# Dealing out the rows of wq, and merging a load and a store, in a decode block bound by its loads

## The chip, the cores and the metric

The kernel runs on one core of a Trainium2 chip. A core has a matrix engine (TensorE, PE in the profile), VectorE (DVE), ScalarE (ACT), GpSimd (POOL) and SyncE (SP), an on-chip memory of 128 partitions (SBUF), accumulators for PE (PSUM), and 16 DMA engines that move data between the chip's main memory (HBM) and SBUF. SP and ACT each have a queue from which they issue DMA transfers. The metric is the time of one execution in microseconds of device time; runs are told by their median.

## The reference

One decode step of a transformer block in float32: two sequences (B = 2), one new token each, model width D = 512, 32 heads of 128, a cache of 8192 keys and values per head, and a gated feed-forward part of width 1792.

```
h  = x + attention(layernorm(x)) @ wo
     q = layernorm(x) @ wq                      (2 x 4096)
     scores = q . k_cache / sqrt(128), softmax over 8192 keys, then . v_cache
h2 = h + (silu(n @ w_gate) * (n @ w_up)) @ w_down,   n = layernorm(h)
```

The caches are 268 MB each, wq and wo 8.4 MB each, and the three feed-forward matrices 3.7 MB each. Every byte is read once, 564.66 MB in all. The output is 2 x 512 numbers.

## The kernel before, in words

There are three large buffers of 128 partitions x 64 KB: two for keys (`kslot`) and one for wq, values and wo (`vslot`). Attention goes in U = 32 rounds, each of two heads of one sequence: 64 partitions per head, 128 keys in each partition. In a round VectorE multiplies the keys by the query in two halves (L419) and sums each product (L428); the maximum is found (L436, L319, L372), ScalarE takes the exponential (L385), and PE multiplies with the values (L329) and sums the pieces (L341).

All loads are issued by SP in one list (`loads`, L142 to L197, issued at L578 to L581): wq, K0 in two halves, K1, V0, K2, V1 and so on, the last values, then wo (three transfers, `WO`), w_gate with w_up (`WF`), and w_down in five pieces (`WD`). A load whose buffer is still in use waits on SP for the last reader of that buffer (`after`, L202 to L206), so the list is strictly in order.

The opening: GpSimd builds the identity matrix `ident` (L209, L213). ScalarE waits for it and then issues the load of x (L219). VectorE builds `fold` and `quarter` from ident, normalizes x (`layernorm`, L233 to L256: statistics, a power on GpSimd, one `tensor_scalar` into `y`), and PE transposes `y` into four columns per sequence (L253). In this transposition the model index is split as (p c), 128 partitions by c = 4, because partition p of wq's buffer holds the four rows 4p to 4p + 3 of wq, 64 KB in one piece. GpSimd then fills its remaining constants (L261 to L268, `consts_done`). When wq has landed, 64 steps of PE compute the queries (L292); the last of these frees `vslot` for V0.

The close: when the last round's output is done, PE gathers the heads (L463) and multiplies with wo, 32 chunks c of 128 rows, in order (L478); before a chunk with which a transfer begins it waits for that transfer (L472 to L474). The residual is added (L487, L491), the sum is normalized again, `hT` receives the transposed rows in the first two of 32 columns (L500), and the gate and up products run with all 32 columns (L512), each waiting for its loads. PE adds the residual h1 to the result through a slice of ident (L530), and multiplies with w_down (L564). Four column blocks t of the result sit in four groups of 32 partitions; in each group the first two partitions are the two sequences. VectorE copies them to SBUF (L575), and two stores, one from SP and one from ACT, write one sequence each (L583 to L592). SP waits for both and clears the semaphores.

Of the kernel before, what the change touches and what calls it, by code (L numbers as in the profile page):

```python
# [5 lines left out]
OP = mybir.AluOpType  # L6
# [3 lines left out]
P = 128  # L10
# [3 lines left out]
class Program:  # L14
# [16 lines left out]
    def wait(self, engine, *points):  # L31
        for s, value in points:
            if self.known[engine].get(s, 0) < value:
                self.known[engine][s] = value
                self.steps[engine].append(lambda e, s=s, v=value: e.wait_ge(s, v))  # L35

    def do(self, engine, fn, sem=None, by=1):

        if sem is None:
            self.steps[engine].append(fn)  # L40
            return None
        self.count[sem] += by
        self.steps[engine].append(lambda e: fn(e).then_inc(sem, by))
        return sem, self.count[sem]
# [8 lines left out]
def decode_block(nc, x, k_cache, v_cache, wq, wo, w_gate, w_up, w_down, out):  # L53
    B, _, D = x.shape
    _, H, S, DH = k_cache.shape
    F = w_gate.shape[1]
    assert DH == P and B == 2 and D == 512 and F == 14 * P and H == 32 and S == 64 * P
    DC = D // P
# [4 lines left out]
    HP = P // 2  # L63
    NJ = S // HP
    U = B * H // 2
    MQ = H // 2
    HALF = (slice(0, HP), slice(HP, P))

# [8 lines left out]
    def sbuf(name, *shape, align=32):  # L77
        return nc.alloc_sbuf_tensor(name, list(shape), F32, align_bytes=align).ap()
# [6 lines left out]
    kslot = [sbuf(f"kslot{n}", P, SLOT, align=512) for n in range(2)]  # L85
    vslot = sbuf("vslot", P, SLOT, align=512)
    xs = sbuf("xs", B, D)
    ident = sbuf("ident", P, P)
    nscale = sbuf("nscale", 1, HP)
    mhalf = sbuf("mhalf", B, 1)  # L90
# [8 lines left out]
    hT = sbuf("hT", P, DC, 32)  # L99
# [13 lines left out]
    mv = sbuf("ln_mv", B, 2)  # L113
    ve = sbuf("ln_ve", B, 1)
    rstd = sbuf("ln_rstd", B, 1)
    y = sbuf("ln_y", B, D)
# [8 lines left out]
    yt = bank[3][:, : DC * B].rearrange("p (c b) -> p c b", b=B)  # L125
    oq_ps = bank[3][:, DC * B : DC * B + B * H].rearrange("p (b c) -> p b c", b=B)
    f_ps = bank[1][:, P : 2 * P]

    g = Program(nc)
    wait, do = g.wait, g.do  # L130


    s_dve, s_act, s_pe, s_pool = (g.sem(n) for n in ("dve", "act", "pe", "pool"))
    s_dve_pe, s_act_pe, s_v = (g.sem(n) for n in ("dve_pe", "act_pe", "v"))
    s_k = [g.sem(f"k{n}") for n in range(2)]

    def alone(name):
        return g.sem(name)
# [5 lines left out]
    loads = []  # L144
# [12 lines left out]
            sem = alone(f"{kind}{i}_{c}") if own else s_k[i % 2] if kind == "k" else s_v  # L157
            loads.append(((kind, i), c, t[:, c * n : (c + 1) * n], k_src(cache, i)[:, c * n : (c + 1) * n], sem))

    loads.append((("wq", 0), 0, vslot, wq.rearrange("(p c) m -> p (c m)", p=P), s_v))  # L160
    load_kv("k", 0, 2)
    for i in range(1, U):
        load_kv("k", i)
# [2 lines left out]


    wo_t = vslot
    WO = ((0, 20), (20, 8), (28, 4))
    for e, (c, n) in enumerate(WO):  # L170
        loads.append((
            ("wo", 0), e,
# [8 lines left out]
    for e, (c, n) in enumerate(WF):  # L181
        src, c0 = (w_gate, c) if c < DC else (w_up, c - DC)
# [20 lines left out]
    for i in range(1, U):  # L203
        after["v", i] = ("v", i - 1) if i < U - 1 else ("k", U - 2)
        if i > 1:
            after["k", i] = ("k", i - 2)  # L206


    p0 = do("gpsimd", lambda e: e.memset(ident, 0.0), s_pool)  # L209
    wait("gpsimd", p0)  # L210
    ident_done = do(
        "gpsimd",
        lambda e: e.affine_select(  # L213
            out=ident, in_=ident, compare_op=OP.not_equal, fill=1.0, base=0, pattern=[[-1, P]], channel_multiplier=1
        ),
        s_pool,
    )
    wait("scalar", ident_done)
    do("scalar", lambda e: e.dma_start(xs, x.rearrange("b s d -> (b s) d")), x_in := alone("x"), 16)  # L219
    p0 = do("gpsimd", lambda e: e.memset(sides, 0.0), s_pool)  # L220
    do("vector", lambda e: e.memset(nscale, -SCALE))
    half_done = do("vector", lambda e: e.memset(mhalf, -0.5), s_dve)
    wait("vector", ident_done)
# [6 lines left out]
    do("vector", lambda e: e.memset(opart, 0.0))  # L230


    def layernorm(src, ready):  # L233
        wait("vector", *ready)
        p = do("vector", lambda e: e.bn_stats(stats, src), s_dve)  # L235
        wait("vector", p)
        p = do("vector", lambda e: e.bn_aggr(mv, stats), s_dve)
        wait("vector", p)
        p = do("vector", lambda e: e.tensor_scalar(ve, mv[:, 1:2], EPS, None, op0=OP.add), s_dve)
        wait("gpsimd", p)  # L240
        p = do("gpsimd", lambda e: e.tensor_tensor(rstd, ve, mhalf, op=OP.pow), s_pool)
        wait("vector", p)
        p = do(
            "vector",
            lambda e: e.tensor_scalar(y, src, mv[:, 0:1], rstd, op0=OP.subtract, op1=OP.mult),
            s_dve,
        )
        normed = p
        wait("tensor", p, ident_done)
        for c in range(DC):  # L250
            p = do(
                "tensor",
                lambda e, c=c: e.transpose(yt[:, c, :], y.rearrange("b (p c) -> b c p", c=DC)[:, c, :], ident[:B, :B]),  # L253
                s_pe if c == DC - 1 else None,
            )
        return normed, p  # L256

    _, p = layernorm(xs, [(x_in, 16)])


    for t, value in (  # L261
        (sides[HALF[0], :, :W], 1.0),
        (sides[HALF[1], :, W:], 1.0),
        (pz, 0.0),
        (hT, 0.0),
    ):
        wait("gpsimd", p0)
        p0 = do("gpsimd", lambda e, t=t, value=value: e.memset(t, value), s_pool)  # L268
    consts_done = p0


    wait("vector", p)
    p = do("vector", lambda e: e.tensor_copy(xT, yt), s_dve)
# [10 lines left out]
    for n, (m, b) in enumerate((m, b) for m in range(0, MQ, 4) for b in range(B)):  # L284
# [3 lines left out]
        for c in range(DC):  # L288
            for k in range(2):
                p = do(  # L290
                    "tensor",
                    lambda e, ps=ps, c=c, k=k, m=m, b=b: e.matmul(  # L292
                        ps[HALF[k]],
                        xb[:, c * B + b, :],
                        wqv[:, c, k, m : m + 4, :],
                        start=(c == 0),
                        stop=(c == DC - 1),
                    ),
# [11 lines left out]
    base = g.count[s_pe]  # L310
# [99 lines left out]
    for i in range(U):  # L410
        m, b = divmod(i, B)
# [3 lines left out]
        for c in range(parts):  # L415
# [7 lines left out]
            if i and c == 1:  # L423
                recip(i - 1)
            wait("vector", mult)
            p = do(
                "vector",
                lambda e, kt=kt, s=scores[i % 2][:, c * n : (c + 1) * n]: e.tensor_reduce(s, kt, axis=AX.X, op=OP.add),  # L428
                s_dve,
            )  # L430
        freed["k", i] = p
        if i:
# [16 lines left out]
    p = do(  # L449
        "vector",  # L450
        lambda e: e.tensor_tensor(  # L451
            om,
            oT.rearrange("p h b -> p b h")[:, :, :, None].to_broadcast([P, B, H, NQ]),
            quarter[:, None, None, :].to_broadcast([P, B, H, NQ]),
            op=OP.mult,
        ),
        s_dve,
    )
    wait("tensor", p)
    for b in range(B):  # L460
        p = do(
            "tensor",
            lambda e, b=b: e.matmul(  # L463
                oq_ps[:, b, :], om[:, b].rearrange("p h q -> p (h q)"), fold, start=True, stop=True
            ),
            s_pe if b == B - 1 else None,
        )
    wait("scalar", p)
    p = do("scalar", lambda e: e.activation(oq.rearrange("p c b -> p b c"), oq_ps, AF.Copy), s_act)
    wait("tensor", p, zeroed)  # L470
    for c in range(H):
        for e_, (c0, n) in enumerate(WO):  # L472
            if c0 == c:
                wait("tensor", landed[("wo", 0), e_])  # L474
        t = c % 4
        p = do(
            "tensor",
            lambda e, c=c, t=t: e.matmul(  # L478
                wide[0][32 * t : 32 * t + B, :],
                oq[:, c, :],  # L480
                wo_t[:, c * D : (c + 1) * D],
                start=(c < 4),
                stop=(c >= H - 4),
            ),
# [4 lines left out]
    p = do("scalar", lambda e: e.activation(osb, wide[0], AF.Copy), s_act)  # L489
# [5 lines left out]
    h1 = rest[:B, :D]  # L495
# [1 line left out]
    wait("scalar", normed)  # L497
    h1_done = do("scalar", lambda e: e.activation(h1, attn, AF.Copy), s_act)
    wait("vector", yt_done)
    hT_done = do("vector", lambda e: e.tensor_copy(hT[:, :, :B], yt), s_dve)  # L500
    wait("tensor", hT_done)

    def project_f(first, ps):
# [20 lines left out]
    p = project_f(0, gate)  # L524

    wait("tensor", h1_done)
    for t in range(4):
        do(
            "tensor",
            lambda e, t=t: e.matmul(  # L530
                f_ps[32 * t : 32 * t + 32, :], ident[:B, :32], h1[:, t * P : (t + 1) * P], start=True, stop=False
            ),
        )
    sg = rest[:, D : D + FQ]
    wait("scalar", p)
    p = do("scalar", lambda e: e.activation(sg, gate, AF.Sigmoid), s_act)
    wait("vector", p)
    sg_done = do("vector", lambda e: e.tensor_mul(sg, gate, sg), s_dve)
    p = project_f(DC, up)
# [4 lines left out]
    p = do(  # L544
        "vector",
        lambda e: e.tensor_mul(
            gu.rearrange("p (c j) -> p j c", c=FB),
            up.rearrange("p (j c) -> p j c", c=FB),
            sg.rearrange("p (j c) -> p j c", c=FB),
        ),  # L550
        s_dve,
    )
    gT = rest[:, D + 2 * FQ : D + 3 * FQ]
    wait("vector", p)
    p = do("vector", lambda e: e.transpose(gT, gu), s_dve)
    wait("tensor", p)
    for c in range(FB):
# [3 lines left out]
        for t in range(4):  # L561
            p = do(
                "tensor",
                lambda e, c=c, t=t: e.matmul(  # L564
                    f_ps[32 * t : 32 * t + 32, :],
                    gT[:, c * 32 : (c + 1) * 32],
                    wd_t[:, c * D + t * P : c * D + (t + 1) * P],
                    start=False,
                    stop=(c == FB - 1),
                ),  # L570
# [7 lines left out]
    for item, e_, dst, src, sem in loads:  # L578
        if item in after:
            wait("sync", freed[after[item]])  # L580
        do("sync", lambda e, dst=dst, src=src: e.dma_start(dst, src), sem, 16)  # L581
    stored = []
    for b, engine in enumerate(("sync", "scalar")):  # L583
        wait(engine, res_done)
        stored.append(
            do(
                engine,
                lambda e, b=b: e.dma_start(out[b, 0, :].rearrange("(t m) -> t m", t=4), res[b::32, :]),
                alone(f"out{b}"),
                16,  # L590
            )
        )  # L592

    wait("sync", *stored)
    ids = sorted(s.num for s in g.sems)
    assert ids == list(range(ids[0], ids[-1] + 1))
    do("sync", lambda e: e.sem_clear(range(ids[0], ids[-1] + 1)))
# [39 lines left out]
```

## Time and profile before

| | us |
|---|---|
| median of 3 runs | 1309.95 (1309.79 to 1310.46) |
| the profiled execution | 1309.7 |
| its span, first to last instruction | 1308.4 |
| DVE busy | 1131.3 (86%) |
| PE busy | 434.1 (33%) |
| ACT busy | 80.4 (6%) |
| mean granted TensorE clock | 0.634 |

A DMA transfer is cut into packets, here one contiguous piece of a partition's row each; the 16 engines work through their packets side by side. A timeline row gives the start, the length, the engine, the line, the operation, the output and inputs, and in brackets how long the engine had been idle and what ended that. A row of DMA issues ends with the size in KB and the time from issue to landing. "SPq" and "ACTq" are the issuing sequencers.

### The profile page before, as it was taken

What the parts mean: (1) busy time and instruction counts of PE and PEld (TensorE: products, weight loads), DVE (VectorE), ACT (ScalarE), POOL (GpSimd) and SP (SyncE); (2) the same over time, 40 slices, a digit from 0 to 9 for tenths busy, and PEclk for the clock granted to TensorE, in tenths of its full rate; (3) what the DMA queues carried; (4) which work ended last, traced back from release to release, by engine and by line L of the source; (5) the groups of instructions that cost most, each with busy time, mean ns of one, the idle gap of its engine ahead of it and who ended that gap; (6) DMA issues with size and microseconds to landing.
All of it is one profiled execution on the core that took longest, in us unless ns stands there. A gap on an engine that the chain in (4) does not pass through costs nothing.

```text
span 1308.4 us, 6704 instructions
## 1 busy us (share of the span) xinstructions
PE 434.1 (33%) x2952; PEld 135.6 (10%) x2952; DVE 1131.3 (86%) x246; ACT 80.4 (6%) x271; POOL 2.9 (0%) x13
## 2 busy tenths in 40 slices
PE   3633223333223333311333321233332233332276
PEld 1210001011001011100101100001100010110022
DVE  1999988889888889988888988888998888898841
ACT  0100000000000000000000000000000000000010
POOL 0000000000000000000000000000000000000000
PEclk9865566666556666656666656666655666665578
DMA  9999999999999999999999999999999999999998
GB/s 403 440 437 439 427 447 423 443 423 445 421 445 425 441 435 431 443 427 443 423 445 421 445 425 441 433 433 443 427 441 425 441 425 441 429 439 435 431 423 371
DMA packets 11118, 564.79 MB, mean 432 GB/s; under 512 B 1242, under 2 KB 1250, under 8 KB 1636
## 3 DMA queue, kind: packets, MB, share of 16 engines
q1 hardware_dynamic: 11096, 564.67, 99.7%
q8 instruction: 5, 0.08, 0.0%
q14 instruction: 5, 0.04, 0.0%
q10 hardware_dynamic: 12, 0.01, 0.0%
HBM read 564.66 MB, written 0.00 MB: 432 GB/s over the span
## 4 chain that ended last, share of the span: by engine, by line
DMA 53%; DVE 45%; PE 1%; SPq 0%; issue 0%; DVEq 0%
DMA kslot<-in_A_k_cache_dram 48%; DVE kslot L419 22%; DVE s L428 22%; DMA kslot<-in_A_v_cache_dram 3%; DMA kslot<-in_B_w_down_dram 3%; PE opart L329 1%; DVE gm L372 0%; SPq L581 0%; DVE r L398 0%; PE bank L564 0%; DVE m L436 0%; DVE kslot L575 0%; DVEq L35 0%
## 5 line engine op out<-in xcount | busy, mean ns | idle before, releaser
L419 DVE TENSOR_TENSOR kslot<-kslot,qsb 128x8192 f32<-128x8192 f32 x64 | 555.6, 8681 | 119.5 <-DMA kslot<-in_A_k_cache_dram 119.5
L428 DVE TENSOR_REDUCE s<-kslot 128x64 f32<-128x8192 f32 x64 | 555.2, 8675 | 0.1
L329 PE MATMUL opart<-vslot,pz 128*8 128x512 f32 x1984 | 285.3, 740 | 246.5 <-DMA vslot<-in_A_v_cache_dram 246.5
L321 PE MATMUL bank<-gm,nscale 1*64 1x1 f32 x64 | 11.8, 250 | 358.4 <-DVE gm L372 358.4
L329 PEld LDWEIGHTS opart<-vslot,pz 128*8 128x8 f32 x1984 | 55.3, 104 | 450.4 <-DMA vslot<-in_A_v_cache_dram 249.1
L319 PE MATMUL bank<-ident,m 128*1 128x128 f32 x64 | 18.7, 395 | 168.1 <-DVE m L436 168.1
L321 PEld LDWEIGHTS bank<-gm,nscale 1*64 1x64 f32 x64 | 9.1, 199 | 374.4 <-DVE gm L372 374.4
L341 PE MATMUL bank<-rdiag,osb 128*128 128x2 f32 x256 | 33.7, 254 | 26.3 <-ACT osb L405 26.3
L400 ACT ACTIVATE rdiag<-fold,r 128x8 f32<-128x8 f32 x32 | 9.6, 301 | 484.6 <-DVE r L398 484.6
L379 ACT ACTIVATE nb<-bank 128x1 f32<-128x1 f32 x32 | 5.5, 171 | 551.6 <-PE bank L322 551.6
L341 PEld LDWEIGHTS bank<-rdiag,osb 128*128 128x128 f32 x256 | 31.0, 191 | 56.0 <-ACT osb L405 56.0
L292 PE MATMUL wide<-vslot,osb 128*64 128x512 f32 x128 | 29.9, 630 | 9.4 <-DMA vslot<-in_A_wq_dram 9.4
L324 PE MATMUL bank<-rs,sides 128*128 128x1 f32 x64 | 18.8, 363 | 41.5 <-ACT pz L385 41.5
L385 ACT ACTIVATE pz<-s,nb 64x128 f32<-64x128 f32 x64 | 25.5, 399 | 1.4
L405 ACT ACTIVATE osb<-opart 128x512 f32<-128x512 f32 x32 | 19.1, 597 | 72.4 <-PE opart L329 72.4
L324 PEld LDWEIGHTS bank<-rs,sides 128*128 128x128 f32 x64 | 16.1, 313 | 44.2 <-ACT pz L385 44.2
L319 PEld LDWEIGHTS bank<-ident,m 128*1 128x1 f32 x64 | 2.7, 81 | 171.6 <-DVE m L436 171.6
L292 PEld LDWEIGHTS wide<-vslot,osb 128*64 128x64 f32 x128 | 10.5, 146 | 28.0 <-issue 28.0
L385 ACT ACTIVATION_READ_ACCUMULATOR pz<-s,nb 64x1 f32 x64 | 11.8, 184 | 0.0
L322 PE MATMUL bank<-gm,nscale 1*64 1x1 f32 x64 | 11.8, 250 | 0.0
L235 DVE BATCH_NORM_STATS2 ln_stats<-attn 2x6 f32<-2x512 f32 x1 | 0.7, 686 | 11.4 <-PE attn L491 11.4
L451 DVE TENSOR_TENSOR om<-oT,quarter 128x256 f32<-128x256 f32 x1 | 0.4, 426 | 11.4 <-ACT oT L407 11.4
(60 smaller groups left out, 104.3 us busy)
## 6 DMA issues: line engine op xcount, KB each, us to landing
kslot<-in_A_k_cache_dram SPq DMA_DIRECT2D x2, 4096.0 KB, 35.8
vslot<-in_A_wo_dram SPq DMA_DIRECT2D x1, 5120.0 KB, 22.0
kslot<-in_B_w_gate_dram SPq DMA_DIRECT2D x1, 3584.0 KB, 31.7
kslot<-in_B_w_up_dram SPq DMA_DIRECT2D x2, 1792.0 KB, 37.5
vslot<-in_A_wo_dram SPq DMA_DIRECT2D x1, 2048.0 KB, 26.4
kslot<-in_B_w_down_dram SPq DMA_DIRECT2D x2, 1024.0 KB, 29.9
vslot<-in_A_wo_dram SPq DMA_DIRECT2D x1, 1024.0 KB, 28.4
kslot<-in_B_w_down_dram SPq DMA_DIRECT2D x1, 768.0 KB, 32.3
```

The source lines that it names most:

```text
L292: lambda e, ps=ps, c=c, k=k, m=m, b=b: e.matmul(ps[HALF[k]], xb[:, c * B + b, :], wqv[:, c, k, m : m + 4, :], start=(c == 0), stop=(c == D ...
L319: e.matmul(mrow, m1, ident, start=True, stop=True).then_inc(s_pe, 1)
L321: e.matmul(nb_ps[HALF[0]], nscale, gm[:, 0:1], start=True, stop=True)
L322: e.matmul(nb_ps[HALF[1]], nscale, gm[:, 1:2], start=True, stop=True).then_inc(s_pe, 1)
L324: e.matmul(den, sides.rearrange("p w a -> p (w a)"), rs, start=True, stop=True).then_inc(s_pe, 1)
L329: inst = e.matmul(opart[32 * t : 32 * t + 2 * W, :], pz[:, w, :], t_v[:, w * W * DH : (w + 1) * W * DH], start=(w < 4), stop=(w >= NW - 4),)
L341: inst = e.matmul(ot_ps, osb[:, a * DH : (a + 1) * DH], rdiag[:, a::W], start=(a == 0), stop=(a == W - 1))
L385: lambda e, k=k, h=h: e.activation(pz[h, :, k * W : (k + 1) * W], s[h].rearrange("p (w a) -> p w a", a=W), AF.Exp, bias=nb[h], scale=SCALE ...
L400: do("scalar", lambda e: e.activation(rdiag, diag, AF.Copy, scale=r))
L405: do("scalar", lambda e: e.activation(osb, opart, AF.Copy), s_act_pe)
L419: mult = do("vector", lambda e, kt=kt, qb=qb: e.tensor_tensor(kt, kt, qb, op=OP.mult), s_dve)
L428: lambda e, kt=kt, s=scores[i % 2][:, c * n : (c + 1) * n]: e.tensor_reduce(s, kt, axis=AX.X, op=OP.add),
```

## The change

- The source of the wq load is described as (i e c) with e = 16 and c = 4: partition 8e + i receives the four rows that begin at row 64i + 4e. Each partition still receives one contiguous piece of 64 KB. If the 16 DMA engines take eight consecutive partitions each, engine e begins 64 KB behind engine e - 1, and goes on 1 MB further at each of its eight rows; before, it began 512 KB behind and read on without a gap.
- To match, the first normalization writes `y` in the order (e i c). The second one is left as it is.
- ScalarE issues the load of x as its first act and no longer waits for ident.
- wo comes in two transfers, chunks 0 to 19 and 20 to 31, instead of three.
- The two sequences sit in columns 0 and 16 of hT's 32 (`LANE` = 16), and so in partitions 0 and 16 of each group of the result. A new constant `place`, built by GpSimd with a memset and a select, puts the residual there. One store from SP, of eight partitions 16 apart, replaces the two.

```diff
+    LANE = 32 // B
+    place = sbuf("place", B, 32)
-    loads.append((("wq", 0), 0, vslot, wq.rearrange("(p c) m -> p (c m)", p=P), s_v))
+    NE = 16
+    loads.append((("wq", 0), 0, vslot, wq.rearrange("(i e c) m -> e i (c m)", e=NE, c=DC), s_v))
-    WO = ((0, 20), (20, 8), (28, 4))
+    WO = ((0, 20), (20, 12))
+    do("scalar", lambda e: e.dma_start(xs, x.rearrange("b s d -> (b s) d")), x_in := alone("x"), 16)
     p0 = do("gpsimd", lambda e: e.memset(ident, 0.0), s_pool)
...
-    wait("scalar", ident_done)
-    do("scalar", lambda e: e.dma_start(xs, x.rearrange("b s d -> (b s) d")), x_in := alone("x"), 16)
     p0 = do("gpsimd", lambda e: e.memset(sides, 0.0), s_pool)
+    p1 = do("gpsimd", lambda e: e.memset(place, 0.0), s_pool)
...
-    def layernorm(src, ready):
+    def layernorm(src, ready, **sizes):
+        into = y.rearrange("b (e i c) -> b i e c", **sizes) if sizes else y
+        from_ = src.rearrange("b (i e c) -> b i e c", **sizes) if sizes else src
...
-            lambda e: e.tensor_scalar(y, src, mv[:, 0:1], rstd, op0=OP.subtract, op1=OP.mult),
+            lambda e: e.tensor_scalar(into, from_, mv[:, 0:1], rstd, op0=OP.subtract, op1=OP.mult),
...
-    _, p = layernorm(xs, [(x_in, 16)])
+    _, p = layernorm(xs, [(x_in, 16)], e=NE, c=DC)
...
+    wait("gpsimd", p1)
+    p0 = do(
+        "gpsimd",
+        lambda e: e.affine_select(
+            out=place, in_=place, compare_op=OP.not_equal, fill=1.0,
+            base=0, pattern=[[-1, 32]], channel_multiplier=LANE,
+        ),
+        s_pool,
+    )
     consts_done = p0
...
-    hT_done = do("vector", lambda e: e.tensor_copy(hT[:, :, :B], yt), s_dve)
+    hT_done = do("vector", lambda e: e.tensor_copy(hT[:, :, ::LANE], yt), s_dve)
...
-                f_ps[32 * t : 32 * t + 32, :], ident[:B, :32], h1[:, t * P : (t + 1) * P], start=True, stop=False
+                f_ps[32 * t : 32 * t + 32, :], place, h1[:, t * P : (t + 1) * P], start=True, stop=False
...
-    stored = []
-    for b, engine in enumerate(("sync", "scalar")):
-        wait(engine, res_done)
-        stored.append(
-            do(
-                engine,
-                lambda e, b=b: e.dma_start(out[b, 0, :].rearrange("(t m) -> t m", t=4), res[b::32, :]),
-                alone(f"out{b}"),
-                16,
-            )
-        )
-    wait("sync", *stored)
+    wait("sync", res_done)
+    rows = out.rearrange("b s (t m) -> t (b s) m", t=4)
+    stored = do("sync", lambda e: e.dma_start(rows, res[::LANE, :]), alone("out"), 16)
+    wait("sync", stored)
```

More of the change, by code (lines that the diff above doesn't have):

```diff
@@ L268, in decode_block @@
         p0 = do("gpsimd", lambda e, t=t, value=value: e.memset(t, value), s_pool)
+    wait("gpsimd", p1)
+    p0 = do(
+        "gpsimd",
+        lambda e: e.affine_select(
+            out=place,
+            in_=place,
+            compare_op=OP.not_equal,
+            fill=1.0,
+            base=0,
+            pattern=[[-1, 32]],
+            channel_multiplier=LANE,
+        ),
+        s_pool,
+    )
     consts_done = p0
```

## The prediction

> **What bounds the kernel now.** I read the page first: the slices of the span, the share of each DMA queue, and the chain that ended last.
>
> ```profile
> DMA  9999999999999999999999999999999999999998
> GB/s 403 440 437 439 427 447 423 443 423 445 421 445 425 441 435 431 443 427 443 423 445 421 445 425 441 433 433 443 427 441 425 441 425 441 429 439 435 431 423 371
> q1 hardware_dynamic: 11096, 564.67, 99.7%
> HBM read 564.66 MB, written 0.00 MB: 432 GB/s over the span
> DMA 53%; DVE 45%; PE 1%; SPq 0%; issue 0%; DVEq 0%
> ```
>
> The chain gives VectorE 45%, but that is only one way through work that waits on loads. The queue row says more: the sixteen DMA engines spend 99.7% of the whole span inside packets of SP's queue. So I cut the span into stretches. The columns are the stretch, its length, busy time by engine, the granted clock, the DMA share and GB/s. This view books a packet's bytes and its whole duration in the stretch where the packet starts, so in a stretch that holds exactly one start of each of the 16 engines the DMA share times the length is the mean duration of a packet.
>
> ```profile
> 100.00:600.00 500.00, 154.45 (x1040) 47.25 (x1040) 458.37 (x93) 28.89 (x104) 0.00 (x0) 0.61 1.00 434
> 600.00:1200.00 600.00, 177.40 (x1208) 55.23 (x1208) 543.08 (x109) 34.50 (x125) 0.00 (x0) 0.61 1.00 434
> 55.00:67.09 12.09, 0.00 (x0) 0.00 (x0) 12.06 (x2) 0.00 (x0) 0.00 (x0) 0.62 0.99 428
> 1.50:2.50 1.00, 0.00 (x0) 0.00 (x0) 0.89 (x3) 0.41 (x1) 0.11 (x1) 1.00 3.21 1049
> 4.50:5.50 1.00, 0.00 (x0) 0.00 (x0) 0.00 (x0) 0.00 (x0) 0.00 (x0) 1.00 2.42 1049
> 7.00:8.00 1.00, 0.00 (x0) 0.00 (x0) 0.00 (x0) 0.00 (x0) 0.00 (x0) 1.00 2.43 1053
> 1.79:1.80 0.01, 0.00 (x0) 0.00 (x0) 0.01 (x2) 0.00 (x0) 0.00 (x0) 1.00 21.67 6554
> 2.04:2.06 0.02, 0.00 (x0) 0.00 (x0) 0.02 (x1) 0.00 (x0) 0.00 (x0) 1.00 9.15 3277
> 2.10:2.20 0.10, 0.00 (x0) 0.00 (x0) 0.04 (x1) 0.10 (x1) 0.00 (x0) 1.00 5.88 1966
> 5.40:5.50 0.10, 0.00 (x0) 0.00 (x0) 0.00 (x0) 0.00 (x0) 0.00 (x0) 1.00 1.51 655
> ```
>
> Between 100 and 1200 us the DMA engines are busy 1.00 of the time at 434 GB/s. There is no hole for a compute step to close. 564.66 MB at 434 GB/s is 1301.1 us of the 1308.4. What is left, some 7 us, is the start, the end, and what the packets lose. That bounds any gain of this change to a few microseconds.
>
> The stretch 1.50 to 2.50 holds 1.049 MB, which is 16 packets of 65.5 KB: the first row of wq on every engine. They take 3.21 us each; the second ones (4.50 to 5.50) take 2.42, as do all later ones. So the start of wq loses 0.79 us per engine, once. Two narrow stretches single out the ends: the packet that starts at 1.79 to 1.80 takes 21.67 x 0.01 x 16 = 3.47 us, the one at 2.04 to 2.06 takes 9.15 x 0.02 x 16 = 2.93 us. Lost time on the DMA engines is lost for good, because nothing behind it is ever idle.
>
> **The change, part by part.**
>
> *wq's rows dealt out.* Same bytes, same 128 rows of 64 KB. Only the addresses at which the engines stand together change: 64 KB apart instead of 512 KB, and each engine then jumps 1 MB from row to row instead of reading on. The trace of before does not show the new pattern, so I bound it. Best: no first packet loses anything. The latest second packet starts in 5.40 to 5.50, while the latest first one starts by 2.20 and would then end by about 4.6: up to 0.9 us. Worst within the aim: nothing changes, 0, because every first packet is slow for being the first. Between: even the fastest lost 2.93 - 2.42 = 0.51, which I call common to a cold start; the part that differs between engines (up to 3.47 - 2.93 = 0.54) looks like engines in each other's way, and this is what other addresses can remove. The latest engine would then start its second packet at about 2.15 + 2.93 = 5.08 instead of about 5.45. I take -0.4 us, nearest to the row of the fastest packet. A loss is possible too and is a rival below.
>
> *x's load moved ahead.* ScalarE no longer waits for ident (its issue at 1.49 follows POOL's select, done at 1.46) and issues at about 0.8, beside SP's issue of wq.
>
> ```profile
> 0.73 0.40 SPq L581 DMA_DIRECT2D vslot<-in_A_wq_dram  x1
> 1.49 0.56 ACTq L219 DMA_DIRECT2D xs<-in_A_x_dram  x1
> 10.40 0.68 DVE L235 BATCH_NORM_STATS2 ln_stats<-xs 2x6 f32<-2x512 f32 x1 [7.75 <-DMA xs<-in_A_x_dram]
> 12.13 0.54 DVE L245 TENSOR_SCALAR ln_y<-xs,ln_mv,ln_rstd 2x512 f32<-2x512 f32 x1 [0.67 <-POOL ln_rstd L241]
> 1.17 0.29 POOL L213 TENSOR_SCALAR_AFFINE_SELECT ident<-ident 128x128 f32<-128x128 f32 x1 [0.24 <-POOL ident L209]
> 13.60 0.43 DVE L278 COPY osb<-xT 128x512 f32<-128x512 f32 x1
> 22.80 29.86 PE L292 MATMUL wide<-vslot,osb 128*64 128x512 f32 x128 [9.44 <-DMA vslot<-in_A_wq_dram]
> 1294.79 0.62 DVE L538 TENSOR_TENSOR kslot<-wide,kslot 128x448 f32<-128x448 f32 x1 [7.15 <-ACT kslot L536]
> 1298.73 0.91 DVE L546 TENSOR_TENSOR kslot<-wide,kslot 128x448 f32<-128x448 f32 x1 [3.32 <-PE wide L512]
> 1306.28 0.65 SPq L588 DMA_DIRECT2D out_dram<-kslot  x1
> 1306.29 0.61 ACTq L588 DMA_DIRECT2D out_dram<-kslot  x1
> ```
>
> Its 4 KB are the difference between 1053 and 1049 in the stretch 7.00 to 8.00; they now come before or among the first packets and cost the same there. Everything up to osb may finish some 7 us earlier, and that is worth nothing: osb is ready at 14.03, and the projection starts at 22.80 because wq lands last. The risk is wq's own issue. Two issues at once took 0.65 and 0.61 at the end, while SP's for wq took 0.40 alone; if ScalarE's goes first, wq starts up to 0.6 us later, and so does everything. At the end SP, 0.01 us ahead, shows no wait for ScalarE. Bounds 0 to +0.6; I take 0.
>
> *y permuted on its way out, place, hT.* The first normalization's last step writes the same 512 elements in another order. A permuted VectorE step of this kernel (L546, 0.91 us) against a plain one of the same size (L538, 0.62) says 1.5 times, so 0.54 becomes about 0.8; it lies in the 8.7 us between osb and wq, so 0. The memset and affine_select of place (L213's select of 128 columns took 0.29) and the later end of POOL's constants are first needed after the projection, at 52.7: 0. The copy into hT moves the same 8 elements per partition, and place has the shape of the slice of ident that it replaces: 0.
>
> *wo in two transfers.* One issue fewer, on a queue that then waits for the last scores anyway. Each engine loses eight 8 KB packets joined to eight 16 KB ones. The cost of a packet as such comes from a stretch with 2 KB packets only:
>
> ```profile
> 1304.62:1305.12 0.50, 0.28 (x12) 0.28 (x16) 0.00 (x0) 0.00 (x0) 0.00 (x0) 1.00 0.23 86
> vslot<-in_A_wo_dram SPq DMA_DIRECT2D x1, 2048.0 KB, 26.4
> vslot<-in_A_wo_dram SPq DMA_DIRECT2D x1, 1024.0 KB, 28.4
> 1250.53 1.28 SPq L581 DMA_DIRECT2D vslot<-in_A_wo_dram  x3
> 1274.05 8.23 PE L478 MATMUL wide<-vslot,oq 128*2 128x512 f32 x64 [0.32 <-ACT oq L469]
> 1279.11 0.10 PEld L478 LDWEIGHTS wide<-vslot,oq 128*2 128x2 f32 x4 [0.33 <-issue]
> 1287.47 0.17 DVE L500 COPY hT<-bank 128x8 f32<-128x8 f32 x1 [0.73 <-PE bank L253]
> 1288.40 5.75 PE L512 MATMUL wide<-kslot,hT 128*32 128x448 f32 x32 [0.97 <-DMA kslot<-in_B_w_gate_dram]
> 1296.89 1.71 PE L512 MATMUL wide<-kslot,hT 128*32 128x448 f32 x16 [0.75 <-DMA kslot<-in_B_w_up_dram]
> 1303.60 0.86 PE L564 MATMUL bank<-kslot 128*32 128x128 f32 x24 [0.77 <-DMA kslot<-in_B_w_down_dram]
> ```
>
> 86 / (0.23 x 16) = 23.4 GB/s per engine, against 434 / 16 = 27.1: 2 KB take 88 ns instead of 76, so about 12 ns per packet, and eight of them 0.1 us. Against it, a new wait on PE. Rows 20 to 27 of wo used to be covered by a transfer that landed at about 1251.0 + 26.4 = 1277.4 (three issues in 1.28, so 0.43 apart); now they wait for the last byte, at about 1251.4 + 28.4 = 1279.8. PE loads c = 20 (weights 41 to 44 of 64) at 1279.11, so it stalls about 0.7 us. Behind it: hT, done at 1287.64, while the gate product starts at 1288.40 because w_gate lands then (0.76 to spare); later w_up holds PE for 0.75 and w_down for 0.77. The stall is swallowed there; without that cover it would cost 0.7. Sum: -0.1, bounds -0.1 to +0.6.
>
> *One store.* The two stores run side by side, but not equally late:
>
> ```profile
> 1307.50:1307.70 0.20, 0.00 (x0) 0.00 (x0) 0.00 (x0) 0.00 (x0) 0.00 (x0) 0.50 0.04 10
> 1307.70:1307.80 0.10, 0.00 (x0) 0.00 (x0) 0.00 (x0) 0.00 (x0) 0.00 (x0) 0.50 0.00 0
> 1307.80:1307.90 0.10, 0.00 (x0) 0.00 (x0) 0.00 (x0) 0.00 (x0) 0.00 (x0) 0.50 0.09 21
> SPq L35 <- DMA out_dram<-kslot: 1.3, 1, 1.3
> ```
>
> 2 KB move between 1307.50 and 1307.70, and 2 KB more after 1307.80, although both were issued within 0.01 us. The later one ends SP's wait of 1.3 us. One store of 4 KB from SP moves with the first: -0.25 us, bounds -0.4 (1307.90 back to 1307.50) to 0 (twice the rows per engine, or a longer issue, could eat it).
>
> Sum against the profiled execution: 1309.7 (span 1308.4 and 1.3 around it) - 0.4 - 0.1 - 0.25 = 1308.95. The median of the runs shown lies 0.25 above that execution, so the forecast for the median is 1309.95 - 0.75 = **1309.2 us**. What a measurement of this kernel tells from no change is about 0.2%, 2.6 us, so this counts as no change.
>
> **Rivals.**
>
> *Nothing at the start.* The first packets are slow because they are first, not for their addresses. For it: all 16 lose at least 0.51 us, and from the second packet on the engines stand the same 512 KB apart and lose nothing (2.42). Against: the loss differs from 0.51 to 1.05 among packets that start within 0.4 us. Then only store and wo stay: 1309.95 - 0.35 = 1309.6. The same comes out if the change doesn't do what it says: that an engine takes eight consecutive partitions is assumed, and if it takes others, the new order still puts engines megabytes apart at the start. [...]
>
> *Slower: the new jumps cost on every row.* If engines in step 64 KB apart, each jumping 1 MB, hinder one another as much as the first packets did, and don't drift apart, all eight rows of wq take 3.21 instead of 2.42: 7 x 0.79 = 5.5 us more, 1309.95 + 5.5 - 0.35 = 1315.1. It decides the sign from 2.6 us, about four slow rows of eight. For it: 3.21 is what engines in step can cost. Against: it heals after one row here. [...]
>
> *x ahead of wq.* ScalarE's issue delays SP's by 0.25 to 0.6 us, at the very point where nothing can make it up: 1309.2 + 0.25 to 0.6, 1309.5 to 1309.8, or 1310.2 where the start gains nothing either.
>
> **How the numbers follow.** Forecast, with a gain of 0.2 to 0.9 at the start: 0.50 (1308.6 to 1309.4). Nothing at the start: 0.30 (1309.5 to 1309.7). x ahead: 0.12 (up to 1310.2). Slower: 0.08, of which nearly all is beyond 2.6 us. To be faster by over 0.2% all bounds together (0.9 + 0.1 + 0.4) fall short by more than 1 us; 0.02 is left for what I have not seen. Which DMA engine is caught by an instruction fetch can shift the last landing by some tenths, so the range is 1308.2 to 1310.5; only the slower rival lies wholly outside.
>
> **What would show it.** Right: in the first microsecond of packets the mean falls from 3.21 to about 2.9, x's statistics start near 3 us, wq's product starts at 22.4 instead of 22.80, one store, and SP's last wait near 1.0. A PE wait on wo of about 0.7 at c = 20, and waits on w_gate shortened by as much. Wrong: first packets at 3.2 again; second and later packets of wq above 2.42; a first packet of wq starting later than 2.20; a DMA share below 1.00 anywhere before 1300.

## The result: 21 us slower, all of it in one load

The changed kernel takes 1330.91 us (median of 5 runs, 1330.75 to 1331.21), the kernel before in the same comparison 1309.79 (1309.66 to 1310.46). The ratio is 1.0161, with a 95% interval of 1.0149 to 1.0172. The forecast was 1309.2, in a range of 1308.2 to 1310.5, with 0.08 for slower; even the slower rival stood at 1315.1. The span of the profiled execution went from 1308.4 to 1329.3, by 20.9.

The page of the changed kernel shows where, in the slices of the span:

```profile
DMA  9999999999999999999999999999999999999998
GB/s 221 348 438 442 414 440 440 438 422 438 438 440 432 426 438 442 438 418 438 442 438 418 438 442 438 418 442 438 438 422 438 436 440 434 426 436 440 442 411 372
```

The DMA engines are still busy from end to end, as before. But the first slice moves 221 GB/s where it moved 403, and the second 348 where it moved 440. Busy engines that move half as much: this is not a hole, it is slow packets. The windows of the changed kernel (columns as in the prediction) single out rows of wq. Each of the first five holds one packet of every engine, so the DMA share is the mean duration in us:

```profile
2.20:3.20 1.00, 0.00 (x0) 0.00 (x0) 0.98 (x2) 0.38 (x1) 0.00 (x0) 1.00 4.76 1049
6.70:7.70 1.00, 0.00 (x0) 0.00 (x0) 0.00 (x0) 0.00 (x0) 0.00 (x0) 1.00 5.09 1049
16.80:17.80 1.00, 0.00 (x0) 0.00 (x0) 0.00 (x0) 0.00 (x0) 0.00 (x0) 1.00 5.09 1049
21.90:22.90 1.00, 0.00 (x0) 0.00 (x0) 0.00 (x0) 0.00 (x0) 0.00 (x0) 1.00 4.93 1049
37.00:38.00 1.00, 0.00 (x0) 0.00 (x0) 0.00 (x0) 0.00 (x0) 0.00 (x0) 1.00 5.08 1049
100.00:600.00 500.00, 153.30 (x1040) 48.00 (x1040) 458.27 (x92) 28.78 (x104) 0.00 (x0) 0.61 1.00 434
```

From the second row on the packets take about 5.1 us, not 2.42, and those of the first row 4.76, not 3.21; the fifth row (21.90, 4.93) is a little faster than its neighbours, which matters below. After wq the engines run at 434 GB/s as ever. The timeline of the changed kernel gives the consequence:

```profile
0.73 0.53 ACTq L212 DMA_DIRECT2D xs<-in_A_x_dram  x1
0.73 0.70 SPq L600 DMA_DIRECT2D vslot<-in_A_wq_dram  x1
2.56 0.62 DVE L240 BATCH_NORM_STATS2 ln_stats<-xs 2x6 f32<-2x512 f32 x1
44.18 30.52 PE L311 MATMUL wide<-vslot,osb 128*64 128x512 f32 x128 [38.72 <-DMA vslot<-in_A_wq_dram]
1301.01 2.76 PE L497 MATMUL wide<-vslot,oq 128*2 128x512 f32 x24 [2.46 <-DMA vslot<-in_A_wo_dram]
1309.58 4.81 PE L531 MATMUL wide<-kslot,hT 128*32 128x448 f32 x32 [0.67 <-DMA kslot<-in_B_w_gate_dram]
1318.01 1.71 PE L531 MATMUL wide<-kslot,hT 128*32 128x448 f32 x16 [1.62 <-DMA kslot<-in_B_w_up_dram]
1327.51 0.68 SPq L603 DMA_DIRECT2D out_dram<-kslot  x1
SPq L607 <- DMA out_dram<-kslot: 1.1, 1, 1.1
```

The projection starts at 44.18 instead of 22.80, 21.4 us late, and nothing behind it can make that up because the loads never pause. By rows: the first packets start at about 2.24 instead of 1.76 (0.5), the first row takes 4.76 instead of 3.21 (1.55), six rows take about 5.09 and one 4.93 instead of 2.42 (18.5). That is 20.6 of the 21.4; the other 0.8 lies between the last packet and the start on PE. The DMA engines lose a little more behind wq: the first 32 KB packets of K0 take 1.69 us (those that start in 42.10 to 43.10), where they took 1.22 before (21.70 to 22.40). So the engines lose 20.6 + 0.5 = 21.1 us, and the median rose by 21.1.

### The profile page after: what moved, and what is told of

It is laid out like the page before. It is cut to its first block, busy times and chain, and to the rows that moved or that the text cites. A ratio compares the mean times of both kernels' runs of the same rounds, so it can differ in the third digit from the quotient of the medians.

```text
span 1329.3 us, 6704 instructions
## 1 busy us (share of the span) xinstructions
PE 431.4 (32%) x2952; PEld 137.1 (10%) x2952; DVE 1131.1 (85%) x246; ACT 80.4 (6%) x271; POOL 3.1 (0%) x15
## 4 chain that ended last, share of the span: by engine, by line
DMA 50%; DVE 45%; another core or an unknown queue 4%; PE 1%; issue 0%; POOL 0%; SPq 0%; DVEq 0%; POOLq 0%
DMA kslot<-in_A_k_cache_dram 45%; DVE kslot L438 22%; DVE s L447 22%; DMA kslot<-in_A_v_cache_dram 3%; DMA kslot<-in_B_w_down_dram 2%; PE opart L348 1%; DVE gm L391 0%; PE bank L583 0%; DVE r L417 0%; SPq L600 0%; PE bank L258 0%; DVE ln_y L250 0%; POOL ln_rstd L246 0%; DVE ln_stats L240 0%
## 5 line engine op out<-in xcount | busy, mean ns | idle before, releaser
L455 DVE TENSOR_REDUCE m<-s 128x1 f32<-128x128 f32 x32 | 9.2, 286 | 1.1
## 6 DMA issues: line engine op xcount, KB each, us to landing
vslot<-in_A_wo_dram SPq DMA_DIRECT2D x1, 3072.0 KB, 29.8
```

## The experiments

In a view that groups starts, a window with N packets of 64 KB has a mean duration of share x length x 16 / N; since N is GB/s x length / 65.5 KB, this is 1049 x share / GB/s. All times per packet below come so from one row. The edits are shown shortened. The probes named e3, e4, e5, e8 and e9 are the kernel before with extra loads ahead of its first one, into buffers that are overwritten later; they leave nothing out. Each probe ran once, and is read by its packets, not by its total time.

### Undoing the dealing, and doing it alone

```diff
e1_wq_back, on the changed kernel:
-    wq.rearrange("(i e c) m -> e i (c m)", e=NE, c=DC)
+    wq.rearrange("(p c) m -> p (c m)", p=P)
-    _, p = layernorm(xs, [(x_in, 16)], e=NE, c=DC)
+    _, p = layernorm(xs, [(x_in, 16)])
e2_wq_only, on the kernel before: the same two lines the other way round,
with the permuting layernorm; x, wo and the stores as before
```

> The changed kernel with only wq's rows put back (128 rows in order, first normalization plain). Theory: the whole loss is the dealing of wq's rows, whose sixteen-wide packets take 5.1 us instead of 2.4 on all eight rows (8 x 2.67 = 21.4 us). Then this run loses those 21.4: about 1309.6, that is the time of before or a few tenths less (store -0.3, wo -0.1, x ahead of wq +0.3 to +0.6). Rival: the early load of x, or the merged transfers, hold part of the loss: then it stays above 1312.

Measured: 1309.64 us against 1309.82 of before, ratio 0.9998 (0.9989 to 1.0007).

> The kernel before with only the dealing of wq's rows (and the matching order of the normalized x). Theory: all of the loss is here, about 1331 (1309.8 + 21.4 - up to 0.5). Rival: the slow rows need x's load just ahead of them or another part of the change: then well below 1325.

Measured: 1330.93 us, ratio 1.0160 (1.0144 to 1.0175).

So the dealing of wq's rows is the whole loss, and everything else in the change together can't be told from nothing.

### Is it the addresses? Eight address patterns

```diff
e3_pitches, on the kernel before, ahead of the loads:
+    for n, (pitch, step) in enumerate([(512,64),(64,1024),(64,64),(512,8192),
+                                       (68,1088),(128,2048),(256,4096),(1024,64)]):   # KB
+        src = AP(k_cache, offset=0, [[pitch, 16], [step, 8], [1, SLOT]])
+        p = do("sync", dma_start(kslot[0], src), alone(f"probe{n}"), 16)
+        wait("sync", p)
```

> The kernel before, with eight extra 8 MB loads of the key cache ahead of the first load, each issued when the one before it has landed. They differ only in the address pattern: the distance of two neighbouring engines / the step from row to row of one engine, in KB: 512/64 (as before), 64/1024 (as the change), 64/64, 512/8192, 68/1088, 128/2048, 256/4096, 1024/64. Time of the kernel is not of interest (some 200 to 300 us longer). Theory A, engines in step at the same offset within 64 KB collide: 64/1024 and 64/64 take 5.1 us per packet, 68/1088 takes 2.4, and 128/2048 and 256/4096 are slow as well or partly. Theory B, sixteen engines that read within one stretch of about 1 MB get half the rate: 64/1024, 64/64 and 68/1088 all take 5.1, 128/2048 about 2.5 to 4, 256/4096 2.4. Theory C, the jump of each engine from row to row costs: 512/8192 and 128/2048 slow, 64/64 at 2.4. And the first packets: if they are slow for being the first, all patterns lose 0.5 us or more in the first row after the idle time; if for their addresses, 512/64 does and 1024/64 or 68/1088 may not.

The windows of this probe, the second row of packets of each pattern in order:

```profile
4.60:5.60 1.00, 0.00 (x0) 0.00 (x0) 0.00 (x0) 0.00 (x0) 0.00 (x0) 1.00 2.43 1049
28.60:29.80 1.20, 0.00 (x0) 0.00 (x0) 0.00 (x0) 0.00 (x0) 0.00 (x0) 1.00 4.26 874
71.20:72.90 1.70, 0.00 (x0) 0.00 (x0) 0.00 (x0) 0.00 (x0) 0.00 (x0) 1.00 3.00 617
115.10:116.30 1.20, 0.00 (x0) 0.00 (x0) 0.00 (x0) 0.00 (x0) 0.00 (x0) 1.00 4.26 874
158.40:159.50 1.10, 0.00 (x0) 0.00 (x0) 0.00 (x0) 0.00 (x0) 0.00 (x0) 1.00 4.64 953
201.20:202.40 1.20, 0.00 (x0) 0.00 (x0) 0.00 (x0) 0.00 (x0) 0.00 (x0) 1.00 4.26 874
244.10:245.20 1.10, 0.00 (x0) 0.00 (x0) 0.00 (x0) 0.00 (x0) 0.00 (x0) 1.00 4.66 953
287.10:288.90 1.80, 0.00 (x0) 0.00 (x0) 0.00 (x0) 0.00 (x0) 0.00 (x0) 1.00 2.85 583
```

1049 x share / GB/s is 2.43 for the first pattern and 5.10 to 5.13 for all seven others, whatever their distances: 64 KB or 1 MB between engines, jumps or none, powers of two or 68 KB. All three address theories fell at once. What the seven share, and the first does not, is the description: 512/64 is one stride over 128 rows, because 512 KB is eight times 64 KB. The seven others are 16 x 8 rows that can't be written as one stride (can't be merged, below).

A new theory, P, had to say what that does: the partitions that the engines write at one time decide, not the addresses that they read. If the rows of a 16 x 8 source go to engines in consecutive runs, engine e fills partitions 8e to 8e + 7, and at one time the engines write partitions 0, 8, 16 and so on; theory P takes it that some of these hold one another up. The faster fifth row (4.93) could belong to that, because there the engines step from partitions 8e + 3 to 8e + 4; this is a guess, since no run singles that step out. The next runs vary the partitions.

### Partitions or description

```diff
e4_ports, ahead of the loads; one row of 64 KB per engine:
+    for step, cut in ((1, 1), (8, 1), (4, 1), (7, 1), (7, 2), (8, 2)):
+        for t in (*kslot, vslot):
+            src = AP(k_cache, n * SLOT, [[8 * SLOT, 16], [128 * SLOT, cut], [1, SLOT // cut]])
+            p = do("sync", dma_start(t[0 : 15 * step + 1 : step], src), alone(f"probe{n}"), 16)
+            n += 1
+        wait for all three
e8_few, the same with few engines:
+    for rows, step in ((2,1),(2,2),(2,4),(2,8),(2,16),(2,32),(2,64),(4,4),(4,11),(4,16),(4,1),(8,4),(8,8)):
+            src = AP(k_cache, n * SLOT, [[8 * SLOT, rows], [1, SLOT]])
+            p = do("sync", dma_start(t[0 : (rows - 1) * step + 1 : step], src), ...)
```

> The kernel before with 18 extra loads of 16 rows of 64 KB (one row per engine, source rows 512 KB apart) ahead of the first load, in groups of three without a wait between them. Only the partitions they are written to differ: every 1st, 8th, 4th, 7th partition from 0, then every 7th and 8th again with the row cut in two so that the source cannot be merged into one stride. [...] Rival S (a source described with an outer dimension of 16 is slow as such): the step makes no difference, or only the cut forms are slow. Rival of addresses: all alike at 2.42.

The windows of this probe, the second of three packets per engine, for partitions 1, 8, 4 and 7 apart:

```profile
9.50:11.50 2.00, 0.00 (x0) 0.00 (x0) 0.00 (x0) 0.00 (x0) 0.00 (x0) 1.00 4.84 524
38.10:39.60 1.50, 0.00 (x0) 0.00 (x0) 0.00 (x0) 0.00 (x0) 0.00 (x0) 1.00 3.42 699
55.90:57.80 1.90, 0.00 (x0) 0.00 (x0) 0.00 (x0) 0.00 (x0) 0.00 (x0) 1.00 2.70 552
73.60:74.70 1.10, 0.00 (x0) 0.00 (x0) 0.00 (x0) 0.00 (x0) 0.00 (x0) 1.00 4.53 953
```

That is 9.7, 5.1, 5.1 and 5.0 us. The pattern of the source is the same in all; only the partitions differ, and the time follows them: four times 2.42 us for partitions 1 apart, about twice for 8, 4 and 7 apart. The groups with the cut forms took no longer from their first issue to the next group's: 17.0 us against 17.1 for 7 apart, 17.8 against 18.5 for 8 apart.

> The kernel before with 39 extra loads of 2, 4 or 8 rows of 64 KB (one row per engine, so 2, 4 or 8 engines at work, always the same kind of source) in 13 groups of three ahead of the first load; only the distance of the partitions they are written to differs. [...] Rival S (the description of the source is slow, not the partitions): no difference between distances.

The windows of e8_few: pairs 2, 4, 32 and 64 apart; then four rows 4 apart, and two windows for the four rows 11 apart, since two of them start early and two late; then eight rows 4 and 8 apart.

```profile
23.40:23.60 0.20, 0.00 (x0) 0.00 (x0) 0.00 (x0) 0.00 (x0) 0.00 (x0) 1.00 3.21 655
39.50:39.70 0.20, 0.00 (x0) 0.00 (x0) 0.00 (x0) 0.00 (x0) 0.00 (x0) 1.00 1.52 655
70.40:70.80 0.40, 0.00 (x0) 0.00 (x0) 0.00 (x0) 0.00 (x0) 0.00 (x0) 1.00 1.57 328
86.20:86.60 0.40, 0.00 (x0) 0.00 (x0) 0.00 (x0) 0.00 (x0) 0.00 (x0) 1.00 0.76 328
96.20:96.50 0.30, 0.00 (x0) 0.00 (x0) 0.00 (x0) 0.00 (x0) 0.00 (x0) 1.00 2.02 874
106.20:107.00 0.80, 0.00 (x0) 0.00 (x0) 0.00 (x0) 0.00 (x0) 0.00 (x0) 1.00 0.38 164
107.00:108.00 1.00, 0.00 (x0) 0.00 (x0) 0.00 (x0) 0.00 (x0) 0.00 (x0) 1.00 0.64 131
172.60:173.10 0.50, 0.00 (x0) 0.00 (x0) 0.00 (x0) 0.00 (x0) 0.00 (x0) 1.00 2.43 1049
183.60:185.20 1.60, 0.00 (x0) 0.00 (x0) 0.00 (x0) 0.00 (x0) 0.00 (x0) 1.00 1.61 328
```

Pairs: 5.1 at 2 apart, 2.43 at 4, 5.0 at 32, 2.43 at 64 (1 apart took 4.8, 8 apart 2.44, 16 apart 2.43). Two engines alone at work halve one another's rate when their partitions are 2 or 32 apart, and not at all when they are 4 or 64 apart. Four rows 4 apart took 2.42, four rows 16 apart, which hold two pairs 32 apart, 5.0, and four rows 1 apart 9.9. Eight rows 4 apart took 2.43, eight rows 8 apart, with four pairs 32 apart, 5.1. Of the four rows 11 apart two took 2.43 and two 5.1, so engines that hold one another up do not by that slow the others at work. Why all sixteen were slow at 7 apart stays open.

### How rows are split over the engines

```diff
e9_split, ahead of the loads:
+    for outer, inner, step in ((8,2,2),(8,2,4),(8,2,1),(8,2,8),(64,1,2),(32,1,4),(128,1,1),(16,8,1)):
+            src = AP(k_cache, n * SLOT, [[8 * SLOT, outer], [17 * SLOT, inner], [1, SLOT]])
+            p = do("sync", dma_start(t[0 : (rows - 1) * step + 1 : step], src), ...)
```

> The kernel before with 24 extra loads in eight groups of three ahead of the first load, to tell how rows are split over the engines. Groups one to four: a source of 8 x 2 rows that cannot be merged (8 engines, two rows each), written to partitions 2, 4, 1 and 8 apart. [...] Rival S (such a source is slow as such): all four slow. Groups five to eight: 64 rows 2 apart in one stride, 32 rows 4 apart in one stride, 128 rows in one stride, and 16 x 8 rows as in the change. [...] If rows go to engines in consecutive runs, 64 rows, 32 rows and 16 x 8 are at 5.1 and only 128 rows in one stride, for which the split must then be another, at 2.42.

The windows of this probe, the eight groups in order:

```profile
5.00:5.70 0.70, 0.00 (x0) 0.00 (x0) 0.00 (x0) 0.00 (x0) 0.00 (x0) 1.00 1.74 755
23.50:24.50 1.00, 0.00 (x0) 0.00 (x0) 0.00 (x0) 0.00 (x0) 0.00 (x0) 1.00 2.36 524
55.10:56.00 0.90, 0.00 (x0) 0.00 (x0) 0.00 (x0) 0.00 (x0) 0.00 (x0) 1.00 2.85 583
87.90:89.20 1.30, 0.00 (x0) 0.00 (x0) 0.00 (x0) 0.00 (x0) 0.00 (x0) 1.00 1.83 403
117.20:118.20 1.00, 0.00 (x0) 0.00 (x0) 0.00 (x0) 0.00 (x0) 0.00 (x0) 1.00 2.46 1049
149.30:150.10 0.80, 0.00 (x0) 0.00 (x0) 0.00 (x0) 0.00 (x0) 0.00 (x0) 1.00 3.02 1311
166.50:167.80 1.30, 0.00 (x0) 0.00 (x0) 0.00 (x0) 0.00 (x0) 0.00 (x0) 1.00 1.86 807
229.50:230.60 1.10, 0.00 (x0) 0.00 (x0) 0.00 (x0) 0.00 (x0) 0.00 (x0) 1.00 4.65 953
```

Consecutive runs would put the engines of the first four groups 4, 8, 2 and 16 partitions apart at one time. A source that can't be merged runs at 2.42 where that is 4 apart (first row), as eight rows 4 apart did in e8_few, and at 4.7 to 5.1 where it is 8, 2 or 16 apart (rows two to four), distances at which e8_few has 5.0 to 5.1 (eight rows 8 apart, two rows 2 apart, four rows 16 apart). So such a source is not slow as such, and its times fit rows that go to engines in consecutive runs. The last four groups use all sixteen engines. Those in one stride run at full rate (2.42 to 2.46), 64 and 32 rows too, against my expectation: consecutive runs would have put their engines 8 apart, so rows in one stride must be split in another way. Only the 16 x 8 form of the change is slow, 5.12; consecutive runs put its engines 8 apart. The last two groups write the same 128 partitions; whether the rows of the source lie in one stride is what sets 2.42 apart from 5.12.

### Addresses with the split left alone

```diff
e5_plain, ahead of the loads:
+    for n, step in enumerate((64, 128, 256, 1024, 2048, 68, 72, 16)):   # KB
+        src = AP(k_cache, 0, [[step, 128], [1, SLOT]])                   # then wait
+    src = AP(k_cache, 0, [[SLOT, 128], [128 * SLOT, 2], [1, SLOT // 2]])
e6_whole_rows, on the changed kernel:
-    vslot, wq.rearrange("(i e c) m -> e i (c m)", e=NE, c=DC)
+    vslot.rearrange("p (c m) -> p c m", c=DC), wq.rearrange("(c p) m -> p c m", p=P)
     (and the first layernorm permutes to match)
```

> The kernel before with nine extra 8 MB loads ahead of the first, each issued when the one before has landed, all with 128 rows in one stride, of 64, 128, 256, 1024, 2048, 68, 72 and 16 KB, and a last one whose rows come in two halves from 8 MB apart. Theory P (partitions decide, not addresses): all at 2.42 us per 64 KB from the second row on, the last one at 1.21 per half. Rival, addresses: large powers of two (1024, 2048) clearly slower, 68 and 72 not. The first row tells on what the start of wq waits: if addresses cause its 0.8 us, it goes at some of these strides; if it is the start after idle time, all lose 0.5 to 0.8.

The windows of e5_plain: the first rows at 64, 128 and 16 KB, then the second rows at 1024 and 2048 KB.

```profile
1.70:2.70 1.00, 0.00 (x0) 0.00 (x0) 0.84 (x3) 0.62 (x1) 0.00 (x0) 1.00 3.00 1049
23.50:24.50 1.00, 0.00 (x0) 0.00 (x0) 0.00 (x0) 0.00 (x0) 0.00 (x0) 1.00 3.14 1049
164.00:165.00 1.00, 0.00 (x0) 0.00 (x0) 0.00 (x0) 0.00 (x0) 0.00 (x0) 1.00 3.28 1049
71.00:72.10 1.10, 0.00 (x0) 0.00 (x0) 0.00 (x0) 0.00 (x0) 0.00 (x0) 1.00 2.56 953
96.90:97.90 1.00, 0.00 (x0) 0.00 (x0) 0.00 (x0) 0.00 (x0) 0.00 (x0) 1.00 2.78 1049
```

Two answers. The first row after idle time loses 0.5 to 0.9 us at strides of 64, 128, 256 and 16 KB (and more at 1024 and 2048 KB, where it takes 3.6 us on average); none of these strides cures it. In e8_few two engines alone, 4 partitions apart, start with packets of 3.12 us on average, so it needs no crowd. It is not a price of every engine's first packet either: in e1_wq_back four of them set out in 2.40 to 2.80 and took 2.56 on average, while the eleven that set out in 1.76 to 2.20 took 3.19. And addresses do matter, though less than partitions: at strides of 1 and 2 MB the second row takes 2.82 and 2.78 us instead of 2.42, while 64, 128, 256, 68, 72 and 16 KB all take 2.42 to 2.43. The last load, whose 128 rows come in two halves from 8 MB apart, took 21.8 us from its issue to the next one (wq of before landed 21.9 after its issue): two strides do no harm while the 128 partitions themselves lie in one.

> The changed kernel with wq's rows dealt out in another way: partition p receives rows p, p + 128, p + 256, p + 384, so the source has 128 rows as its outer dimension, and neighbouring engines begin near each other and jump 2 MB after each 16 KB. Theory P: no loss of 21 us, since the outer dimension stays 128 and the engines keep their partitions: about 1309.8 (1309.6 plus 24 more packets per engine at some 10 ns). Rival, addresses: jumps of 2 MB or starts near one another cost, 1315 or more.

Measured: 1309.75 us against 1309.93, ratio 0.9999 (0.9990 to 1.0008). This version deals out the rows as well, over 128 rows as the outer dimension, and shows no loss. It shows no gain either.

### What is left of the change

```diff
e7_x_late, on the kernel of e1_wq_back:
-    do("scalar", dma_start(xs, ...))            # as ScalarE's first act
+    wait("scalar", ident_done)
+    do("scalar", dma_start(xs, ...))            # where it was before
```

> The changed kernel with wq's rows put back and x's load where it was (after ident): what is left is one store and wo in two transfers. Expected 1309.4, 0.2 to 0.4 below before (store -0.3, wo -0.1), and 0.2 below the same kernel with x's load first, where the first packets of wq set out up to 0.9 us apart instead of 0.4. Rival: x's place makes no difference, then the same time as that run (1309.64).

Measured: 1309.65 us against 1309.93, ratio 0.9998 (0.9989 to 1.0007). It is the same as with x first (1309.64). The projection on wq starts at 22.84 here and in e1_wq_back, so the 0.2 us expected from x's place did not come. One store and two transfers of wo are worth 0.2 to 0.3 us by the medians, within what the intervals leave open.

## Why the prediction was wrong

**What bounds the kernel: right, and it made the loss whole.** The DMA engines are never idle behind wq either (a share of 1.00 from 100 to 600 us in the changed kernel), so the 21.1 us that they lose at wq and just behind it end up in the time whole.

**wq's rows: wrong, at its first sentence.** "Same bytes, same 128 rows of 64 KB. Only the addresses at which the engines stand together change." The description of the load changed too, from one stride over 128 rows to 16 x 8, and with it which partitions the engines write at one time. e3_pitches shows that the addresses do not decide; e8_few and e9_split show that the partitions do, and the times of unmerged sources (2.42 and 4.7 to 5.1) fit a split in consecutive runs. The term of -0.4 measured +21.1 (e2_wq_only against before). The range missed because both its ends were taken from the first row of before, where nothing of the new split could be seen. No run shows an instruction fetch that shifts the last landing by some tenths, the other ground of the range: the page of before has ten packets of that kind, 0.0% of the queues' time, and its five runs lie 0.8 us apart. The picture of the load before was wrong as well: the description of the change and the prediction let engine e take eight consecutive partitions, 512 KB behind one another. Consecutive runs of eight fit the changed load (5.1); rows in one stride run at 2.42 and so must be split in another way.

**The rival that the change doesn't do what it says: near, and not followed up.** It called eight consecutive partitions per engine an assumption, and drew from that only that the addresses would not be as meant. The question it left out was what partitions the engines would write under the new description, and whether they could all be written at once.

**The slower rival: right in sign, wrong in mechanism and size.** It had all eight rows slow, as they are, but through addresses, at 3.21 us each. They take 5.1 because of the partitions that the engines write at one time: eight rows 8 apart, read from 512 KB behind one another, took 5.1 in e8_few. What addresses alone do is less: by estimate from e5_plain, 2.82 us at 1 MB would cost 0.4 x 8 = 3.2 us. And the pitch between rows of the changed load is not what slows it: e3_pitches has 5.1 for seven different address patterns. (The chances listed with the rivals add up to 1.00 without the 0.02 that is said to be left.)

**Nothing at the start: this rival was right that addresses don't decide.** The part of the excess that differs between engines (up to 0.54) was read as engines in each other's way. The excess is there with two engines alone (3.12 us), and at strides from 16 to 2048 KB (0.5 to 1.2 us). That a packet is slow for being its engine's first is not quite it, though, since late ones lose little (2.56 us in e1_wq_back); why the start of a load is slow stays open.

**x ahead of wq: 0, as taken.** x's statistics start at 2.56, near the 3 that was forecast, the permuted write of y takes 0.54 (not the 0.8 worked out), and in e1_wq_back SP still needs 0.40 us for wq's issue. What did lengthen the issue is the 16 x 8 source: 0.70 us in the changed kernel, 0.70 in e2_wq_only where x comes late; and in the changed kernel the first packets start 0.5 us later.

**wo: the mechanism was right, the wait was larger.** PE waits 2.46 us at c = 20 instead of the 0.7 worked out. Its first 40 steps took 4.47 us, where they had taken 5.06 (1274.05 to 1279.11), and the second transfer landed 29.8 us after its issue, 1.4 more than the 28.4 taken over from before. As said, w_gate (a wait of 0.67) and w_up (1.62) still land later and swallow it.

**One store: right in the profile, too small to show in the time.** SP's last wait fell from 1.3 to 1.1, and from the issue of the store to the end of the span it takes 1329.3 - 1327.5 = 1.8 us instead of 1308.4 - 1306.3 = 2.1; e2_wq_only, with two stores, needs 1329.7 - 1327.75 = 1.95.

## What to carry to other kernels

A change of the address pattern of a load can change which partitions its engines write at one time; ask first whether the source can still be written as one stride over the partitions, because here only loads of 32 rows and more in one such stride kept all sixteen engines at about 2.42 us per 64 KB. In a profile, DMA engines that stay busy at half the usual GB/s, with packets of equal size that take about a whole multiple of their usual time (5.1 and 9.7 us for 2.42), point here to the partitions written at one time rather than to addresses. Where rows must be dealt out, keep the partitions as the outer dimension and rearrange inside a partition, as e6_whole_rows does.

## What the runs showed of the hardware that was not expected

- Two engines that write partitions 1, 2 or 32 apart take 4.8 to 5.1 us per 64 KB, and 2.43 to 2.44 when these are 4, 8, 16 or 64 apart (e8_few); rows 1 apart take 9.9 by fours (e8_few) and 9.7 by sixteens (e4_ports).
- Rows in one stride run at 2.42 to 2.46, also when there are only 32 or 64; rows that need two strides take 5.12 (16 x 8) and 2.42 or 4.7 to 5.1 (8 x 2, by the distance of the partitions), as if they went to the engines in consecutive runs (e9_split).
- The 64 KB packets that set out first after idle time cost 0.5 to 1.2 us extra (e5_plain), 0.7 with two engines alone (e8_few); four that set out in 2.40 to 2.80 in e1_wq_back cost 0.14 on average.
- Strides of 1 and 2 MB between the partitions' rows cost 15 to 17% on the second row (2.82 and 2.78 us, e5_plain). Loads at 256 KB and below lose nothing here (2.42 to 2.43).
- Open: sixteen rows 7 partitions apart are slow on all engines (5.0 us, e4_ports), although of four rows 11 apart only two are slow (5.1 and 2.43, e8_few).
